# Attention with soft mixture of experts on one core: logits one period later and ahead of the scores, the flip of x inside the values, the first exponentials ahead of the copies of P

## The chip, the core and the metric

The kernel runs on one core of a Trainium2 chip. The core has a matrix engine (TensorE, PE in the profile; its weight loads are PEld), three engines for elementwise work (VectorE is DVE, ScalarE is ACT, GpSimd is POOL), and SyncE (SP), which here only issues transfers. Each engine runs its own queue in order; the engines wait for each other by semaphores. Matrix products land in PSUM, whose banks are few and are used in turns. The metric is the time of one execution in microseconds, as the median of several; all times below are in microseconds unless marked.

## The reference

Windowed causal attention over 8 batches, 8 heads, 576 positions of 64 features, then a soft mixture of 8 experts with 4 slots each over the 4608 tokens of 512 features:

```python
scores = scale * q @ k.T;  scores = where((rel >= 0) & (rel < 128), scores - slope[h] * abs(rel), -1e9)
attn = exp(scores - max);  attn /= sum(attn) + 1e-9
x = (attn @ v)                       # rows (b, s), columns (h, d): 4608 x 512
logits = x @ phi                     # 4608 x 32
d = exp(logits - logits.max(0));  d /= d.sum(0) + 1e-9
slot_input = d.T @ x                 # 32 x 512
slot_out[e] = maximum(slot_input[e] @ w1[e], 0) @ w2[e]
c = exp(logits - logits.max(1)); c /= c.sum(1) + 1e-9
out = c @ slot_out
```

## The kernel before

Attention is cut into 36 tiles, numbered k, of 128 query positions, in two groups g = 0 and 1 of 64, for all 8 heads in four pairs. `tiles[k]` is (b, t); t = 0 is the first tile of a batch. Such a tile sees fewer keys (its scores are shorter) and has no second part in its values. They are k = 0, 4, 9, 13, 18, 22, 27 and 35.

One loop runs over k. Every engine's order is the order in which this loop writes its instructions (`manual_schedule`); nothing is moved by a scheduler. The loop is software-pipelined: in period k TensorE works on tiles k-1, k-2, k-3 and k+1. The steps, by the names of the code:

- `scores(k+1, g)`: slope rows (L233) and products of q and k (L246) into the PSUM tile of group g.
- `chain(k, g)` on VectorE: `merge` (L260), `rowmax` (L267), `bias` (L272); it makes `nb`, the bias of the exponentials.
- `expo(k, g)` on ScalarE: four exponentials (L284) that write P of group g to `p4s[g]`.
- `flip(k-1, g)`: four transposes of P (L303) into bank a for g = 0 and bank b for g = 1. In the text, "flips of P" are the two together.
- `take(k-1, g)` on ScalarE: the copy of the flipped P from that bank (L306). `split(k-1, g)` on GpSimd then makes its two masked parts with four selects (L319, L322).
- `values(k-2)`: the first part (L335) multiplies the main blocks of P with v into banks e and o; the second part (L345) adds the corner blocks and closes the sums.
- `x_store(k-2)` on VectorE: row sums, reciprocal, product (L356, L357, L359); writes one of six x tiles.
- `x_flip(k-3)`: four transposes of x (L365) into bank a, the bank that the flipped P of group 0 is copied out of. `x_keep(k-3)` on ScalarE copies them out (L368) to one of four tiles.

Every four tiles make a round q of the mixture. It is spread over the periods by `do(when, k, ...)`, which puts a step at a named place of period k: `logits` (L375, bank b) of the four kept tiles, `token_copy` on ScalarE (L381), `token_max` on VectorE (L386, L388, L390), `token_exp` on ScalarE (L397, L402); a period later `token_sum` (L408), `token_flips` on TensorE (L416, `dp`), `token_keep` on ScalarE (L422, `dn`), `slot_sum` on TensorE (L428, `ap`), `slot_add` on VectorE (L438); `slots_max` and `slots_norm` give small VectorE steps (L450 to L463) to a list of fillers, of which up to four are taken at the end of each period, ahead of the next chain; `slots_exp` is on ScalarE (L455). The places in a period come in the order turn, turn2, keep, x_keep, mid, post, act, dve, late.

After the loop the last tiles are finished, and the experts' two layers and the output follow; the change leaves that part as it was.

Of the kernel before, what the change touches and what calls it, by code (L numbers as in the profile page):

```python
# [25 lines left out]
NPAIR = H // 2  # L26
# [6 lines left out]
NQ = NTT // 4  # L33
# [32 lines left out]
def tile_attn_softmoe(  # L66
# [82 lines left out]
    st = {}  # L149
    last = B - 1  # L150

    def order(b):
        return (1, 2, 3, 4, 0) if b == last else range(4 + b % 2)

    tiles = [(b, t) for b in range(B) for t in order(b)]
# [9 lines left out]
    def bank(tag, shape, name):  # L165
        return ps_1.tile(shape, F32, tag=tag, name=name)
# [84 lines left out]
    def window(k, g, us, o, w):  # L251
        s = st[k, g]
        if isinstance(us, int):
            return s["parts"][us // 2][:, us % 2, o:o + w]
        if s["s4"] is None:
            return s["parts"][us.start // 2][:, :, o:o + w]
        return s["s4"][:, us, o:o + w]

    def merge(k, g, us=ALL):
        nc.vector.copy_predicated(  # L260
            window(k, g, us, 0, KB), bc(mask_le, 1, len(range(4)[us])), window(k, g, us, P, KB))
# [12 lines left out]
    def corner(k, g, par):  # L274
        return par if tiles[k][1] == 4 else g ^ par

    def expo(k, g, us=ALL):
        s = st[k, g]
        s["p4"] = p4s[g]
        for u in range(4)[us]:  # L280
            dst = s["p4"][:, u].rearrange("p (a w) -> p a w", a=2)
            if corner(k, g, u // 2):
                dst = dst[:, ::-1]
            nc.scalar.activation(  # L284
                dst, window(k, g, u, 0, P).rearrange("p (a w) -> p a w", a=2), AF.Exp,
                bias=s["nb"][:, u:u + 1], scale=SCALE)
# [3 lines left out]
    def filler():  # L290
        if fillers:
            fillers.pop(0)()

    def chain(k, g):
        merge(k, g)
        rowmax(k, g)
        bias(k, g)
# [7 lines left out]
    def take(k, g, copy):  # L305
        copy(pas[k % 2][:, g].rearrange("p a j m -> p (a j m)"), st[k, g]["pt"].rearrange("p u w -> p (u w)"))  # L306
# [18 lines left out]
    def values(k, to=None):  # L325
        b, t = tiles[k]
        x = st["x", k] = to or [bank(tag, [P, NPAIR, VD], "xp") for tag in ("e", "o")]
        for j in range(NPAIR):
            for par in range(2):
                for g in range(2):  # L330
                    if t == 4:
                        v = (v3_even, v_slot[b, 3])[g]
                    else:
                        v = v_slot[b, t - 1 + g if t else 0]
                    nc.tensor.matmul(  # L335
                        x[par][half[g], j], lhsT=pas[k % 2][:, g, par, j], rhs=v[:, par, j],
                        start=(j == 0), stop=(t == 0 and j == NPAIR - 1))
        if t == 0:
            return
        for j in range(NPAIR):  # L340
            for par in range(2):
                for g in range(2):
                    rows = half[corner(k, g, par)]
                    v = (v4_even, v4_odd)[g] if t == 4 else v_slot[b, t - g]
                    nc.tensor.matmul(  # L345
                        x[par][half[g], j], lhsT=pps[k % 2][rows, g, j], rhs=v[rows, par, j],
                        start=False, stop=(j == NPAIR - 1))
# [181 lines left out]
    def do(when, k, fn, *a):  # L529
        todo.setdefault((when, k), []).append((fn, a))  # L530

    def run(when, k):
        for fn, a in todo.pop((when, k), []):
            fn(*a)
# [30 lines left out]
            load_v_tails(b + 1)  # L565

    for q in range(NQ - 1):
        k = 4 * q + 3
        do("post", k + 3, logits, q)
        do("act", k + 3, token_copy, q)  # L570
        do("dve", k + 3, token_max, q)
        do("late", k + 3, token_exp, q)
        do("dve", k + 4, token_sum, q)
        do("turn2", k + 4, token_flips, q)
        do("keep", k + 4, token_keep, q)
        do("mid", k + 4, slot_sum, q, "b")
        do("dve", k + 4, slot_add, q)
        do("dve", k + 4, later, slots_max, q)
        do("act", k + 5, slots_exp, q)
        do("dve", k + 5, later, slots_norm, q)  # L580
    for k in range(n - 3):
        do("turn", k + 3, x_flip, k)
        do("x_keep", k + 3, x_keep, k)
# [1 line left out]
    with tc.manual_schedule(engines=ORDERED):  # L585
        scores(0, 0)
        scores(0, 1)
        loads(0)
        for k in range(n):
            if k:  # L590
                chain(k, 0)
            else:
                for us in (LO, HI):
                    merge(k, 0, us)
                    rowmax(k, 0, us)
                    bias(k, 0, us)
                    expo(k, 0, us)
            chain(k, 1)
            if k:
                flip(k - 1, 0, "a")  # L600
                flip(k - 1, 1, "b")
                run("turn", k)
                run("turn2", k)
            if k:
                take(k - 1, 0, nc.scalar.copy)
                split(k - 1, 0)
                load_weights_at(k, 1)
                take(k - 1, 1, nc.scalar.copy)
                split(k - 1, 1)
                load_weights_at(k, 2)  # L610
                expo(k, 0)
            run("keep", k)
            expo(k, 1)
            run("x_keep", k)
            if k >= 2:
                values(k - 2)
                after_values(k - 2)
            run("mid", k)
            if k + 1 < n:
                scores(k + 1, 0)  # L620
                scores(k + 1, 1)
                loads(k + 1)
            if k == n - 2:
                load_weight()
            run("post", k)
            if k >= 2:
                x_store(k - 2)
            run("act", k)
            run("dve", k)
            run("late", k)  # L630
            for _ in range(4):
                filler()

        ka, kb, kc = n - 3, n - 2, n - 1
        lp = free[3]
        idle = inp.bitcast(BF16)[:, 0:512]

        def spin(m):
            if "spin" not in st:
                st["spin"] = bank("o", [P, 512], "spin")  # L640
            for _ in range(m):
                nc.tensor.matmul(st["spin"], lhsT=idle[:, 0:P], rhs=idle, start=True, stop=True)

        for _ in range(3):
            load_weight()
        nc.gpsimd.memset(inp, 0.0)
        flip(kc, 0, "a")
        flip(kc, 1, "b")
        take(kc, 0, nc.scalar.copy)
        take(kc, 1, nc.vector.tensor_copy)  # L650
        x_flip(ka)
        x_keep(ka)
        values(kb)
        for _ in range(5):
            load_weight()
        values(kc, [x.rearrange("p (j d) -> p j d", d=P)[:, :, 0:VD] for x in (free[0], free[2])])
        x_store(kb)
        run("act", n)
        run("dve", n)
        x_store(kc, (0,))  # L660
        x_store(kc, (1,))
        drain()
        for _ in range(2):
            load_weight()
        spin(1)
        turn(0, "a", free[1])
        x_flip(kb, bank("b", [P, DM], "xq"))
        x_keep(kb)
        spin(1)
        x_flip(kc, None, range(0, 2))  # L670
        x_flip(kc, None, range(2, 4))
        x_keep(kc, nc.scalar.copy, slice(0, 2))
        x_keep(kc, nc.vector.tensor_copy, slice(2, 4))
        logits(final, range(3), to=lp)
        logits(final, range(3, 4))
        spin(2)
        load_weight()
        load_weight()
        token_max(final, lp[:, 0:P])
        lane_rows()  # L680
        turn(1, "v", free[1])
        spin(1)
        token_exp(final, lp[:, 0:P])
        lane_exp()
        token_flips(final, (1,))
        token_keep(final, nc.vector.tensor_copy, slice(0, 1))
        token_sum(final)
        spin(1)
        lane_flip()
        slot_sum(final, "e")  # L690
        lane_keep()
        nc.scalar.copy(lg[:, 0:P], lp[:, 0:P])
        load_weight()
        load_weight()
        for cols in (slice(0, DM // 2), slice(DM // 2, DM)):
            slot_add(final, cols)
        spin(3)
        for part in range(2):
            slot_inputs(part)
            inputs_keep(part)  # L700
        lane_sum()
        lane_norm()
        token_flips(final, (0,))
        token_keep(final, nc.scalar.copy, slice(1, 2))
        assert not todo and loaded[0] == NW + len(place), (todo, loaded, len(place))
# [232 lines left out]
```

## Time and profile before

| what | us |
|---|---|
| median of 3 runs (lowest, highest) | 291.5 (290.72, 293.64) |
| the profiled execution's own time | 293.59 |
| its span, first to last instruction | 291.9 |
| TensorE busy in the span | 253.2 |
| VectorE, ScalarE, GpSimd busy | 178.9, 158.2, 97.6 |

The granted TensorE clock is 0.994 of full speed over the span. In the page, a group of instructions is shown by line, engine, operation, and out<-in by the program's names; in a timeline row the columns are start, duration, engine, line, operation, names and shapes, how many instructions are merged into the row, and in brackets the engine's idle time before it with the instruction that ended it. A row of the view of waits gives the total, the number of times and the longest. A row of the view by windows gives the stretch, its length, then each engine's busy time in the order PE, PEld, DVE, ACT, POOL, the clock, the transfers' share and rate. The engines' lines in the rows are those of the kernel before.

### The profile page before, as it was taken

How to read it: one execution, taken by the hardware profiler on the slowest of the kernel's cores; microseconds unless marked ns; L12 is line 12 of the kernel's file. 1: busy time of each engine (PE TensorE's matmuls, PEld its weight loads, DVE VectorE, ACT ScalarE, POOL GpSimd, SP SyncE). 2: the span in 40 equal slices, each digit the busy share in tenths (PEclk: the TensorE clock that was granted, in tenths of full speed). 3: DMA queues.
4: the chain of work that ended last, by engine and by line, in shares of the span. 5: the costliest groups of instructions: out<-in, count | busy, mean ns of one | idle time of the engine just before them, and what ended most of it. 6: DMA issues, size and time to landing. Idle time of an engine off the chain costs nothing.

```text
span 291.9 us, 12240 instructions
## 1 busy us (share of the span) xinstructions
PE 253.2 (87%) x5088; PEld 183.5 (63%) x5088; DVE 178.9 (61%) x550; ACT 158.2 (54%) x481; POOL 97.6 (33%) x269
## 2 busy tenths in 40 slices
PE   7688898988989897898899989989979889999980
PEld 3466776776777586666667757767766532566640
DVE  3566566775794875589478577657865741224461
ACT  2567756666755776656667566866565201013350
POOL 0046344541660566045417541645544001000000
PEclk9999999999999999999999999999999999999997
DMA  6769975788688477668776858855755999998895
GB/s 177 233 223 273 387 255 170 257 248 269 197 288 285 143 252 236 213 199 268 266 246 189 277 178 260 261 186 154 246 168 183 307 395 305 409 372 308 342 384 234
DMA packets 30715, 74.74 MB, mean 256 GB/s; under 512 B 3650, under 2 KB 5698, under 8 KB 30660
## 3 DMA queue, kind: packets, MB, share of 16 engines
q1 hardware_dynamic: 29940, 73.48, 75.5%
q8 instruction: 40, 0.66, 0.9%
q10 hardware_dynamic: 720, 0.48, 0.6%
q14 instruction: 15, 0.12, 0.1%
HBM read 64.51 MB, written 9.44 MB: 253 GB/s over the span
## 4 chain that ended last, share of the span: by engine, by line
PE 64%; DVE 14%; ACT 14%; issue 4%; DMA 1%; ACTq 0%; DVEq 0%
PE s L246 11%; PE xp L335 10%; PE xq L365 6%; ACT area L306 6%; PE op L772 5%; PE xp L345 5%; ACT area L284 5%; PE hp L736 5%; PE pt L303 5%; PE s L233 4%; PE po L793 4%; DVE nb L267 3%; PE lp L375 3%; PE ap L428 3%; DVE s L260 2%
## 5 line engine op out<-in xcount | busy, mean ns | idle before, releaser
L284 ACT ACTIVATE area<-s,nb 128x128 f32<-128x128 f32 x288 | 81.3, 393 | 9.5 <-DVE nb L272 8.2
L322 POOL TENSOR_SCALAR_AFFINE_SELECT area<-area 64x256 f32<-64x256 f32 x112 | 46.4, 414 | 116.1 <-ACT area L306 110.5
L306 ACT COPY area<-pt 128x512 f32<-128x512 f32 x71 | 38.0, 585 | 46.8 <-PE pt L303 46.0
L246 PE MATMUL s<-kq 64*64 64x192 f32 (+2 forms) x1088 | 53.7, 314 | 0.8 <-DMA kq<-k_t 0.8
L267 DVE TENSOR_REDUCE nb<-s 128x4 f32<-128x512 f32 (+1 forms) x73 | 49.9, 684 | 2.6
L319 POOL TENSOR_SCALAR_AFFINE_SELECT area<-area 64x256 f32<-64x256 f32 x112 | 46.1, 412 | 7.5
L246 PEld LDWEIGHTS s<-kq 64*64 64x64 f32 x1088 | 40.2, 138 | 3.8 <-DMA kq<-k_t 1.4
L335 PE MATMUL xp<-va,area 128*64 128x66 f32 x1120 | 40.9, 225 | 1.1 <-issue 1.1
L335 PEld LDWEIGHTS xp<-va,area 128*64 128x64 f32 x1120 | 35.7, 137 | 7.2 <-issue 4.0
L303 PE MATMUL pt<-unit_r,area 128*128 128x128 f32 x288 | 39.7, 280 | 0.6 <-DVE acc L438 0.6
L365 PE MATMUL xq<-unit_r,xs 128*128 128x128 f32 x144 | 23.7, 286 | 18.1 <-ACT area L306 17.0
L303 PEld LDWEIGHTS pt<-unit_r,area 128*128 128x128 f32 x288 | 30.7, 141 | 10.8 <-issue 7.9
L260 DVE COPY_PREDICATED s<-cst,s 128x256 f32<-128x256 int32 (+1 forms) x73 | 30.7, 420 | 9.1 <-PE s L246 8.9
L356 DVE TENSOR_SCALAR rs<-xp 128x4 f32<-128x4 f32 x70 | 8.7, 161 | 39.8 <-PE xp L345 36.4
L233 PE MATMUL s<-ramp 64*64 64x384 bf16 x288 | 26.5, 342 | 6.5 <-ACT area L284 5.6
L365 PEld LDWEIGHTS xq<-unit_r,xs 128*128 128x128 f32 x144 | 15.3, 141 | 26.2 <-ACT area L306 24.8
L359 DVE TENSOR_TENSOR xs<-xp,rs 128x256 f32<-128x256 f32 x70 | 26.5, 420 | 1.2
L368 ACT COPY xs<-xq 128x512 f32<-128x512 f32 (+1 forms) x36 | 22.7, 631 | 1.1 <-PE xq L365 1.0
L233 PEld LDWEIGHTS <-ramp 64*64 64x64 bf16 x288 | 11.6, 107 | 17.3 <-issue 15.8
L799 DVE COPY ob<-po 128x384 f32<-128x384 f32 x24 | 12.3, 553 | 13.1 <-PE po L793 12.5
L345 PE MATMUL xp<-va,area 64*64 64x66 f32 x896 | 19.6, 224 | 0.0
L799 ACT COPY ob<-po 128x384 f32<-128x384 f32 x24 | 10.3, 482 | 13.6 <-PE po L793 13.6
(112 smaller groups left out, 254.5 us busy)
## 6 DMA issues: line engine op xcount, KB each, us to landing
w<-w SPq DMA_DIRECT2D x49, 512.0 KB, 5.5
va<-v_n SPq DMA_DIRECT2D x36, 264.0 KB, 4.8
out<-ob SPq DMA_DIRECT2D x24, 384.0 KB, 4.1
kq<-q_t SPq DMA_DIRECT2D x35, 256.0 KB, 3.8
kq<-k_t SPq DMA_DIRECT2D x32, 256.0 KB, 4.3
xs<-w SPq DMA_DIRECT2D x5, 512.0 KB, 6.5
area<-w SPq DMA_DIRECT2D x4, 512.0 KB, 8.2
kt<-k_t SPq DMA_DIRECT2D x4, 384.0 KB, 5.2
```

The costliest lines, as they stand in the source:

```text
L233: nc.tensor.matmul(parts[par][half[c], :, 0:WIN], lhsT=slope[rows, c], rhs=steps[rows, 0 if t else 1 + g], start=True, stop=False)
L246: nc.tensor.matmul(parts[par][half[c], jh, KB * o:WIN], lhsT=qt[rows, j], rhs=keys, start=False, stop=(jh == 1))
L260: nc.vector.copy_predicated(window(k, g, us, 0, KB), bc(mask_le, 1, len(range(4)[us])), window(k, g, us, P, KB))
L267: nc.vector.tensor_reduce(s["nb"][:, 4 + us.start:4 + us.stop], window(k, g, us, 0, P), axis=AX.X, op=ALU.max, negate=True)
L284: nc.scalar.activation(dst, window(k, g, u, 0, P).rearrange("p (a w) -> p a w", a=2), AF.Exp, bias=s["nb"][:, u:u + 1], scale=SCALE)
L303: nc.tensor.transpose(s["pt"][:, u], s["p4"][:, u], ident)
L306: copy(pas[k % 2][:, g].rearrange("p a j m -> p (a j m)"), st[k, g]["pt"].rearrange("p u w -> p (u w)"))
L319: nc.gpsimd.affine_select(dst, pa, [[0, NPAIR], [-1, KB]], ALU.is_gt, 0.0, base=0, channel_multiplier=1)
L322: nc.gpsimd.affine_select(dst, pa, [[0, NPAIR], [1, KB]], ALU.is_ge, 0.0, base=0, channel_multiplier=-1)
L335: nc.tensor.matmul(x[par][half[g], j], lhsT=pas[k % 2][:, g, par, j], rhs=v[:, par, j], start=(j == 0), stop=(t == 0 and j == NPAIR - 1))
L345: nc.tensor.matmul(x[par][half[g], j], lhsT=pps[k % 2][rows, g, j], rhs=v[rows, par, j], start=False, stop=(j == NPAIR - 1))
L365: nc.tensor.transpose(st["xq", k][:, P * j:P * j + P], xns[k % NXN][:, P * j:P * j + P], ident)
```

## The change

Three edits in the loop:

1. `values` is cut in two functions. The first part now stands directly behind the flips of P; `x_flip` (and `token_flips`) follow it, and then the second part, `values_ex`. `x_keep` moves behind the place "mid".
2. `expo(k, 0)` is written ahead of both `take(k-1, g)` in place of behind them.
3. For the rounds q = 0 to 6 every step is one period later, and `logits` goes from "post" (behind the scores) to "mid" (ahead of them). Round 7 keeps its periods and its place.

```diff
+    def values_ex(k):
+        b, t = tiles[k]
+        x = st["x", k]
+        for j in range(NPAIR if t else 0):
...
     for q in range(NQ - 1):
-        k = 4 * q + 3
-        do("post", k + 3, logits, q)
-        do("act", k + 3, token_copy, q)
...
+        k = 4 * q + 6 + (q < NQ - 2)
+        do("mid" if q < NQ - 2 else "post", k, logits, q)
+        do("act", k, token_copy, q)
...
                 flip(k - 1, 1, "b")
-                run("turn", k)
-                run("turn2", k)
+            if k >= 2:
+                values(k - 2)
+            run("turn", k)
+            run("turn2", k)
             if k:
+                expo(k, 0)
                 take(k - 1, 0, nc.scalar.copy)
                 split(k - 1, 0)
                 load_weights_at(k, 1)
                 take(k - 1, 1, nc.scalar.copy)
                 split(k - 1, 1)
                 load_weights_at(k, 2)
-                expo(k, 0)
             run("keep", k)
             expo(k, 1)
-            run("x_keep", k)
             if k >= 2:
-                values(k - 2)
+                values_ex(k - 2)
                 after_values(k - 2)
             run("mid", k)
+            run("x_keep", k)
             if k + 1 < n:
                 scores(k + 1, 0)
...
         values(kb)
+        values_ex(kb)
```

The changed file has two more lines above the lines named here, so L345 is L347 there, L365 is L367, L368 is L370, L375 is L377.

TensorE, an ordinary period; the rows are line, operation, out<-in and shape, with how many follow each other (`pt` is the flipped P, `xq` the flipped x, `xp` the values, `s_0` and `s_1` the scores of the two groups). One piece of the difference:

```order
 L246 MATMUL s_1_87<-kq 64x192 x8
 L303 MATMUL pt<-unit_r,area 128x128 x8
-L365 MATMUL xq<-unit_r,xs 128x128 x4
-L335 MATMUL xp<-va,area 64x66 x16
-L345 MATMUL xp<-va,area 64x66 x16
+L335 MATMUL xp<-va,area 64x66 x16
+L367 MATMUL xq<-unit_r,xs 128x128 x4
+L347 MATMUL xp<-va,area 64x66 x16
 L233 LDWEIGHTS ramp
```

The flip of x stood between the flips of P and the values; it now stands between the values' two parts.

ScalarE, an ordinary period and the start of the next one, before (`s_0`, `s_1`: exponentials of group 0 and 1; `area<-pt`: the two copies of P; `xs<-xq`: x_keep):

```order
L306 COPY area<-pt 128x512 x2
L284 ACTIVATE area<-s_0_86,nb 128x128 x2
L284 ACTIVATE area<-s_0_86,nb 128x2x64 x2
L284 ACTIVATE area<-s_1_87,nb 128x2x64 x2
L284 ACTIVATE area<-s_1_87,nb 128x128 x2
L368 COPY xs<-xq 128x512
```

and now:

```order
L284 ACTIVATE area<-s_0_86,nb 128x128 x2
L284 ACTIVATE area<-s_0_86,nb 128x2x64 x2
L306 COPY area<-pt 128x512 x2
L284 ACTIVATE area<-s_1_87,nb 128x2x64 x2
L284 ACTIVATE area<-s_1_87,nb 128x128 x2
L370 COPY xs<-xq 128x512
```

The two copies went from ahead of the exponentials of group 0 to behind them.

ScalarE, a round of the mixture, now (`lg<-lp`: the logits' copy, `lg,sb` and `al`: token_exp, `dn<-dp`: token_keep); before, the first copy row stood directly behind `al` and ahead of the exponentials of `s_0`:

```order
L370 COPY xs<-xq 128x512
L383 COPY lg<-lp 128x128
L399 ACTIVATE lg,sb<-lg,nm 128x128
L404 ACTIVATE al<-fine,nm 128x1
L284 ACTIVATE area<-s_0_86,nb 128x128 x2
L284 ACTIVATE area<-s_0_86,nb 128x2x64 x2
L306 COPY area<-pt 128x512 x2
L424 COPY dn<-dp 128x256
```

The logits' copy and its exponentials keep their places between x_keep and the next period's work; what follows them is now the exponentials of group 0 and not the copies.

More of the change, by code (lines that the diff above doesn't have):

```diff
@@ L337, in values @@
                         start=(j == 0), stop=(t == 0 and j == NPAIR - 1))
-        if t == 0:
-            return
-        for j in range(NPAIR):
+    def values_ex(k):
+        b, t = tiles[k]
+        x = st["x", k]
+        for j in range(NPAIR if t else 0):
             for par in range(2):
@@ L567, in tile_attn_softmoe @@
     for q in range(NQ - 1):
-        k = 4 * q + 3
-        do("post", k + 3, logits, q)
-        do("act", k + 3, token_copy, q)
[L571 to L580, printed above, removed]
+        k = 4 * q + 6 + (q < NQ - 2)
+        do("mid" if q < NQ - 2 else "post", k, logits, q)
+        do("act", k, token_copy, q)
+        do("dve", k, token_max, q)
+        do("late", k, token_exp, q)
+        do("dve", k + 1, token_sum, q)
+        do("turn2", k + 1, token_flips, q)
+        do("keep", k + 1, token_keep, q)
+        do("mid", k + 1, slot_sum, q, "b")
+        do("dve", k + 1, slot_add, q)
+        do("dve", k + 1, later, slots_max, q)
+        do("act", k + 2, slots_exp, q)
+        do("dve", k + 2, later, slots_norm, q)
     for k in range(n - 3):
```

## The prediction

> **What bounds the kernel now.** I read the page first, then the waits, then the stretches of one group of four tiles, then the timeline inside them. All steps below are from the start of one instruction group to the start of the next, in us.
>
> The page gives TensorE most of the span. The view of waits gives who waits for whom (total, times, longest): TensorE's flip of x (`x_flip`) waits for ScalarE's copies of P (`take`), and ScalarE's copies wait for TensorE's flips of P.
>
> ```profile
> PE 253.2 (87%) x5088; PEld 183.5 (63%) x5088; DVE 178.9 (61%) x550; ACT 158.2 (54%) x481; POOL 97.6 (33%) x269
> ACT area L306 <- PE pt L303: 46.0, 27, 2.8
> PE xq L365 <- ACT area L306: 17.0, 33, 1.3
> ```
>
> The view by windows, cut at the starts of `x_flip` (which stands once in each period from k = 3 to 35), gives the four stretches of one group: with logits at the end, with slot sums, with the normalising of the slots, plain. The last row is from the first `x_flip` (k = 3) to the last in the loop (k = 35).
>
> ```profile
> 187.04:194.37 7.33, 6.04 (x148) 4.96 (x149) 3.45 (x14) 4.46 (x16) 3.41 (x9) 1.00 0.89 291
> 194.37:201.07 6.70, 6.40 (x127) 4.50 (x127) 5.21 (x16) 3.90 (x13) 3.40 (x9) 1.00 0.48 135
> 201.07:206.38 5.31, 5.02 (x117) 4.16 (x117) 3.73 (x14) 3.84 (x13) 3.41 (x9) 1.00 0.48 143
> 206.38:211.88 5.50, 5.21 (x116) 4.18 (x116) 4.72 (x15) 3.83 (x12) 3.40 (x9) 1.00 0.76 250
> 23.04:218.59 195.55, 173.84 (x3847) 136.76 (x3847) 137.44 (x431) 127.84 (x398) 88.89 (x241) 1.00 0.74 236
> ```
>
> A group takes 24.84 and TensorE is busy in 22.67 of it. The timeline of the third stretch shows the order that makes its 5.31:
>
> ```profile
> 200.43 1.07 ACT L306 COPY area<-pt 128x512 f32<-128x512 f32 x2 [2.80 <-PE pt L303]
> 201.07 0.66 PE L365 MATMUL xq<-unit_r,xs 128*128 128x128 f32 x4 [0.29 <-ACT area L306]
> 201.08 0.41 POOL L322 TENSOR_SCALAR_AFFINE_SELECT area<-area 64x256 f32<-64x256 f32 x1 [2.76 <-ACT area L306]
> 201.65 1.15 PE L335 MATMUL xp<-va,area 128*64 128x66 f32 x32
> 202.74 0.70 PE L345 MATMUL xp<-va,area 64*64 64x66 f32 x32
> 203.25 0.34 PE L233 MATMUL s<-ramp 64*64 64x384 bf16 x4
> 203.40 0.67 ACT L368 COPY xs<-xq 128x512 f32<-128x512 f32 x1
> 203.47 0.25 DVE L356 TENSOR_SCALAR rs<-xp 128x4 f32<-128x4 f32 x2 [1.31 <-PE xp L345]
> 203.87 0.40 ACT L455 ACTIVATE ln<-ln 128x128 f32<-128x128 f32 x1
> 204.07 0.34 PE L233 MATMUL s<-ramp 64*64 64x384 bf16 x4
> 204.61 0.41 POOL L322 TENSOR_SCALAR_AFFINE_SELECT area<-area 64x256 f32<-64x256 f32 x1
> 204.66 0.28 DVE L460 TENSOR_REDUCE cs<-ln 128x4 f32<-128x128 f32 x1
> 204.99 0.85 PEld L303 LDWEIGHTS pt<-unit_r,area 128*128 128x128 f32 x8 [0.28 <-issue]
> 205.60 0.42 DVE L260 COPY_PREDICATED s<-cst,s 128x256 f32<-128x256 int32 x1
> ```
>
> TensorE: x_flip to values .58, values' first part to second 1.09, second part to scores .51, scores .82 and .92, flips of P to the next x_flip 1.39 (at 206.38). Without its wait of .29 that is 5.02. The chain of VectorE and ScalarE runs beside it and ends in time, because ScalarE copies P before it takes up the exponentials. So TensorE and the small wait behind the copy set an ordinary period.
>
> **Copies behind the first exponentials.** The first copy of P now stands in ScalarE's queue behind the four exponentials of group 0 of the next tile, and these need VectorE's chain of that group. The rows for that link, and then the timeline around logits and slot sums:
>
> ```profile
> 106.31 0.42 DVE L260 COPY_PREDICATED s<-cst,s 128x256 f32<-128x256 int32 x1
> 107.75 1.14 ACT L284 ACTIVATE area<-s,nb 128x128 f32<-128x128 f32 x4 [0.23 <-DVE nb L272]
> ...
> 117.63 1.08 PE L375 MATMUL lp<-xs,phi 128*32 128x128 f32 x32
> 118.78 0.27 ACT L381 COPY lg<-lp 128x128 f32<-128x128 f32 x1 [3.41 <-PE lp L375]
> 119.66 0.42 DVE L260 COPY_PREDICATED s<-cst,s 128x256 f32<-128x256 int32 x1
> 120.43 1.05 ACT L306 COPY area<-pt 128x512 f32<-128x512 f32 x2
> 121.04 0.66 PE L365 MATMUL xq<-unit_r,xs 128*128 128x128 f32 x4 [1.29 <-ACT area L306]
> 121.37 1.15 ACT L284 ACTIVATE area<-s,nb 128x128 f32<-128x128 f32 x4
> 121.53 0.43 PE L416 MATMUL dp<-unit_r,lg 128*128 128x128 f32 x2
> 121.89 1.15 PE L335 MATMUL xp<-va,area 128*64 128x66 f32 x32
> 122.38 0.40 ACT L422 COPY dn<-dp 128x256 f32<-128x256 f32 x1
> 123.61 1.07 PE L428 MATMUL ap<-xs,dn 128*32 128x512 f32 x8
> 123.74 0.25 DVE L356 TENSOR_SCALAR rs<-xp 128x4 f32<-128x4 f32 x2 [1.46 <-PE xp L345]
> 124.60 0.36 PE L233 MATMUL s<-ramp 64*64 64x384 bf16 x4
> 124.93 0.21 DVE L408 SCALAR_TENSOR_TENSOR fine<-fine,al,sb 128x1 f32<-128x1 f32 x1
> 126.24 0.42 DVE L260 COPY_PREDICATED s<-cst,s 128x256 f32<-128x256 int32 x1
> ```
>
> This closes a ring through four engines' queues that was open before. x_flip needs bank a, so it waits for the copy; the values' second part is now behind x_flip; `x_store` on VectorE needs that second part; the next chain is behind x_store in VectorE's queue; the exponentials need the chain; the copy is behind the exponentials. Its length in an ordinary period: x_flip to second part .58 (taken from x_flip to values, the nearest row: four transposes and one change of array shape), second part to x_store .73 (202.74 to 203.47), x_store to the next VectorE group 1.19 (203.47 to 204.66), chain to exponentials 1.44 (106.31 to 107.75), four exponentials to the next ScalarE copy 1.01 (121.37 to 122.38), copy to x_flip .64 (200.43 to 201.07): **5.59**.
>
> **x_flip between the values' parts.** TensorE alone would come round in .58 + .51 + .82 + .92 for x_flip to flips of P, then 8 transposes .85 and .17 for the change of shape, then the first part 1.01 and at most .28 (the gap before the flips, 204.99): 5.14. So the move hides 1.29 of the copy's lateness, but the ring is .45 longer than that, and x_flip waits again: what was late .29 is now late .45. The added change of array shape has no row of its own. The link from x_flip to the second part lies in the ring; its bounds are .42 with no gap (over 31 stretches 5.0 less) and .69 with the .28 gap (3.4 more), and I take .58, the row with the same weights before it. The gap from the first part to x_flip lies under the wait and costs nothing; if that wait went, it would cost up to .28.
>
> The Trainium skill (TensorEngine Tiling (Array Packing), Tiling Modes, Key Properties) says that changing the tiling mode, not just the tile, drains TensorE; this speaks against the change, since each period gets one more such change. The gaps in the trace (.17, .28) agree with it in kind; by it the sum stays as below, and with no drain at that place it would be .16 x 31 = 5.0 less.
>
> **GpSimd.** Its eight selects per tile end 4.59 after the first copy starts (200.43 to 204.61 + .41), and the next values' first part needs them. With the copy at x_flip - .64 that is 3.95 + .1 for the signal, so the first part may start at 4.05 and x_flip 1.29 later, at 5.34. That is under 5.59, and shows only where the ring is shorter (k = 6).
>
> **Logits a period later, before the scores.** Removed: the wait of 1.29 before x_flip (.29 + 1.0) behind the logits' copy and exponential on ScalarE, 8 times before, now 7 of them. Added: logits stand between second part and scores, `x_keep` on ScalarE waits for them since it overwrites their input, the logits' copy is behind x_keep, `token_max` on VectorE behind that copy, and the next chain behind token_max. Ring: .58, then .63 to the logits (as for slot sums: 121.89 to 123.61 less 1.09), 1.15 to their end (117.63 to 118.78), x_keep .47 (203.40 to 203.87), copy to chain .88 (118.78 to 119.66), 1.44, 1.01, .64: 6.80 against 7.33 before. Where the tile in the values is the first of its batch it has no second part, and it is .63 less, 6.17 (k = 11 and 15).
>
> **What VectorE does between x_store and the next chain** was beside TensorE's work before and is in the ring now. Slot sums: x_flip to token flips .49, to second part .36, .73, x_store 1.19, `token_sum`, `slot_add` and two fillers 1.31 (124.93 to 126.24), 1.44, 1.01, .64: 7.17 against 6.70. x_store's multiply there now waits for the slot sum that reads the tile it overwrites; if for the first of four, nothing, if for all, .5: I take nothing, as the tile is the first one's. Normalising: 5.59 and .94 for four fillers (204.66 to 205.60): 6.53 against 5.31. Plain: 5.59 against 5.50.
>
> **Sum.** 31 stretches from k = 3 to 34: 9 plain or without extras x 5.59 = 50.3; k = 6, 5.34; logits 5 x 6.80 + 2 x 6.17 = 46.3; slot sums 7 x 7.17 = 50.2; normalising 7 x 6.53 = 45.7: 197.9. The stretch from k = 34 keeps its logits behind scores of 1.11:
>
> ```profile
> 214.07 0.34 PE L233 MATMUL s<-ramp 64*64 64x384 bf16 x4
> 215.18 1.08 PE L375 MATMUL lp<-xs,phi 128*32 128x128 f32 x32
> ```
>
> .58 + .51 + 1.11 + 1.15 + .88 + 1.44 + 1.01 + .64 = 7.3. Together 205.2 against 195.55: +9.7. At the two ends the first part of the values only changes sides of an x_flip (+1.0 before the first, -1.09 behind the last): -.1. The profiled execution took 293.59 (span 291.9 and 1.7 around it), so it becomes 303.2; it was 2.1 above the median of 291.5, so I expect **301.1**. Loads, weights and the tail of experts are untouched.
>
> **Rivals.** (a) TensorE stays the pace. If the chain were ready .45 earlier in an ordinary period and 1.4 earlier in a normalising one, x_flip would find its copy done, and a group would be 4 x 5.14 + .27 (token flips) + 1.11 (slot sums: .63 + .99 - .51) + 1.11 (logits alike) = 23.05 against 24.84. Over 31/4 groups that is -13.9: 278 us. The 1.29 and .29 rows speak for it, the ring against: every link of it is a queue's order or a measured step. It decides from the ring falling below 5.14. The Trainium skill (Perfetto Trace Analysis, Optimization Strategy) says to find the gaps on the busiest engine and make what they wait for start sooner, by which this change should gain; no run here shows yet whether it does.
> (b) Little changes. With no gap behind x_flip (-5.0) it is 296; another .1 off each of 31 turns (-3.1), for instance in the step from exponentials to copy, which I have from the copy of another tile (122.38), gives 293. For it speaks that no row shows x_flip ahead of the second part; against it that the two nearest rows have gaps.
> (c) Worse still: the .5 at slot sums (7 x .5 = 3.5) and .11 more per change of shape (31 x .11 = 3.4): 308. For it speaks the added wait itself, against it that only one of the four slot sums reads the tile.
>
> **Chances.** A measurement of this kernel tells 1% from no change. Forecast with its own range of 296 to 306: .68; (c) .10; (b) .10; (a) and parts of it .12. So faster .12, same .10, slower .78. The range for 8 in 10 takes in (b) and (c): 290 to 308.
>
> **What would show it.** Right: ScalarE's copies no longer wait for TensorE (46.0 falls near 0), its first exponentials wait for the bias instead, x_flip's wait for the copy grows from 17.0 to 20 to 30, and the normalising stretch is above 6.3. The logits stretch shrinks by about .5 in any case. Wrong: x_flip's wait under 10, or VectorE starting a chain sooner than 1.9 after the values' second part in a plain period.

## The result, and the profile after

| | median us (lowest to highest, runs) | profiled execution | its span |
|---|---|---|---|
| before | 291.83 (290.72 to 293.64, 4) | 293.59 | 291.9 |
| after | 308.56 (308.02 to 308.88, 4) | 308.68 | 306.9 |

The change makes the kernel slower: ratio 1.0565, 95% interval 1.0508 to 1.0622. The forecast was 301.1 with a range up to 308.0: the direction and the ring came out, the size did not, and the time lies .56 above the range. Medians here and below are over all runs of a kernel and ratios over its fast ones, which matters for two kernels below: without the runs of a slower state of the chip, 275.12 would be 274.34, and 309.88 would be 308.62.

The page and the view of waits of the kernel after (engine and line waited for, total us, times, longest):

```profile
PE 257.8 (84%) x5086; PEld 186.3 (61%) x5088; DVE 175.9 (57%) x550; ACT 158.4 (52%) x481; POOL 97.6 (32%) x269
L306 ACT COPY area<-pt 128x512 f32<-128x512 f32 x71 | 38.8, 614 | 1.5 <-PE pt L303 1.5
ACT area L284 <- DVE nb L272: 58.7, 27, 3.2
PE xq L367 <- ACT area L306: 31.9, 30, 1.9
DVE xs L361 <- PE ap L430: 7.5, 7, 2.6
```

The copies of P, which waited 46.0 for TensorE, now wait 1.5: by the time ScalarE reaches them the flips are long done. ScalarE waits 58.7 for the bias of the exponentials instead, and x_flip waits 31.9 for the copies where it waited 17.0. The last row is new: x_store's product waits for the slot sums.

The view by windows of the kernel after, cut at the starts of x_flip: one group from k = 23 (logits, slot sums, normalising, plain), then k = 3 to 35 as before.

```profile
151.42:158.23 6.81, 6.16 (x149) 4.95 (x149) 4.53 (x17) 4.60 (x16) 0.00 (x0) 1.00 1.02 376
158.23:165.92 7.69, 5.84 (x95) 3.93 (x95) 4.55 (x12) 4.00 (x13) 3.40 (x9) 1.00 0.50 169
165.92:172.56 6.64, 5.03 (x116) 4.18 (x116) 4.48 (x15) 3.83 (x13) 3.40 (x9) 1.00 0.46 141
172.56:178.31 5.75, 4.76 (x116) 3.96 (x116) 3.68 (x11) 3.63 (x12) 3.40 (x9) 1.00 0.72 254
23.55:233.44 209.89, 175.90 (x3849) 138.30 (x3847) 135.08 (x431) 127.37 (x398) 88.46 (x241) 0.99 0.68 221
```

The loop from the first x_flip to the last takes 209.89 against 195.55, 14.3 of the 15.0 that the span grew by; the start (+.5) and the tail (+.2) hold the rest. The last stretch of that group, by the timeline, shows the ring link by link:

```profile
172.56 0.66 PE L367 MATMUL xq<-unit_r,xs 128*128 128x128 f32 x4 [1.61 <-ACT area L306]
173.15 0.56 PEld L347 LDWEIGHTS xp<-va,area 64*64 64x64 f32 x32 [0.17 <-issue]
173.91 0.25 DVE L358 TENSOR_SCALAR rs<-xp 128x4 f32<-128x4 f32 x2 [1.85 <-PE xp L347]
175.10 0.42 DVE L260 COPY_PREDICATED s<-cst,s 128x256 f32<-128x256 int32 x1
176.57 0.89 PEld L335 LDWEIGHTS xp<-va,area 128*64 128x64 f32 x26 [0.42 <-POOL area L322]
176.63 1.15 ACT L284 ACTIVATE area<-s,nb 128x128 f32<-128x128 f32 x4 [2.12 <-DVE nb L272]
177.65 1.09 ACT L306 COPY area<-pt 128x512 f32<-128x512 f32 x2
178.31 0.42 PEld L367 LDWEIGHTS xq<-unit_r,xs 128*128 128x128 f32 x4 [0.85 <-ACT area L306]
```

x_flip to second part .59, to x_store .76, to the chain 1.19, to the exponentials 1.53, to the copy 1.02, to x_flip .66: 5.75. Each engine starts at once when the one before it has ended, and VectorE, ScalarE and TensorE each sit idle for part of every turn (1.85, 2.12, and .85 in the last row). GpSimd's selects delay the values (.42 at 176.57), but the weight loads of x_flip still wait .85 behind them for the copy, so the selects set nothing here.

### The profile page after: what moved, and what is told of

Read it like the earlier page. It is cut to its first block, busy times and chain, and to the rows that moved or that the text cites. A ratio compares the mean times of both kernels' runs of the same rounds, so it can differ in the third digit from the quotient of the medians.

```text
span 306.9 us, 12376 instructions
## 1 busy us (share of the span) xinstructions
PE 257.8 (84%) x5086; PEld 186.3 (61%) x5088; DVE 175.9 (57%) x550; ACT 158.4 (52%) x481; POOL 97.6 (32%) x269
## 4 chain that ended last, share of the span: by engine, by line
PE 49%; DVE 23%; ACT 17%; issue 7%; POOL 1%; DMA 1%; ACTq 0%; DVEq 0%; POOLq 0%
ACT area L284 10%; PE xq L367 7%; PE xp L347 6%; DVE nb L267 6%; PE op L777 5%; ACT area L306 5%; PE s L246 5%; PE hp L741 5%; PE po L798 4%; DVE xs L361 4%; PE ap L430 3%; PE pt L303 3%; DVE s L260 3%; PE lp L377 3%; PE xp L335 2%
## 5 line engine op out<-in xcount | busy, mean ns | idle before, releaser
L284 ACT ACTIVATE area<-s,nb 128x128 f32<-128x128 f32 x288 | 83.9, 389 | 75.5 <-DVE nb L272 58.7
L322 POOL TENSOR_SCALAR_AFFINE_SELECT area<-area 64x256 f32<-64x256 f32 x112 | 46.3, 414 | 130.7 <-ACT area L306 125.1
L246 PE MATMUL s<-kq 64*64 64x192 f32 (+2 forms) x1088 | 54.8, 319 | 0.7 <-DMA kq<-k_t 0.7
L267 DVE TENSOR_REDUCE nb<-s 128x4 f32<-128x512 f32 (+1 forms) x73 | 49.9, 684 | 2.6
L367 PE MATMUL xq<-unit_r,xs 128*128 128x128 f32 x144 | 23.7, 287 | 31.9 <-ACT area L306 31.9
L319 POOL TENSOR_SCALAR_AFFINE_SELECT area<-area 64x256 f32<-64x256 f32 x112 | 46.1, 412 | 7.8 <-POOL w L146 0.3
L335 PE MATMUL xp<-va,area 128*64 128x66 f32 x1120 | 42.9, 226 | 1.3 <-POOL area L322 0.8
L335 PEld LDWEIGHTS xp<-va,area 128*64 128x64 f32 x1120 | 37.0, 137 | 8.2 <-issue 5.2
L306 ACT COPY area<-pt 128x512 f32<-128x512 f32 x71 | 38.8, 614 | 1.5 <-PE pt L303 1.5
L367 PEld LDWEIGHTS xq<-unit_r,xs 128*128 128x128 f32 x144 | 15.3, 141 | 36.3 <-ACT area L306 36.0
L370 ACT COPY xs<-xq 128x512 f32<-128x512 f32 (+1 forms) x36 | 22.4, 621 | 5.5 <-PE lp L377 4.7
L347 PE MATMUL xp<-va,area 64*64 64x66 f32 x896 | 20.2, 228 | 0.0
L347 PEld LDWEIGHTS xp<-va,area 64*64 64x64 f32 x896 | 16.2, 137 | 4.8 <-issue 4.7
L233 PEld LDWEIGHTS <-ramp 64*64 64x64 bf16 x288 | 10.5, 110 | 13.8 <-issue 13.1
```

What stands on the lines that cost most here:

```text
L246: nc.tensor.matmul(parts[par][half[c], jh, KB * o:WIN], lhsT=qt[rows, j], rhs=keys, start=False, stop=(jh == 1))
L267: nc.vector.tensor_reduce(s["nb"][:, 4 + us.start:4 + us.stop], window(k, g, us, 0, P), axis=AX.X, op=ALU.max, negate=True)
L284: nc.scalar.activation(dst, window(k, g, u, 0, P).rearrange("p (a w) -> p a w", a=2), AF.Exp, bias=s["nb"][:, u:u + 1], scale=SCALE)
L319: nc.gpsimd.affine_select(dst, pa, [[0, NPAIR], [-1, KB]], ALU.is_gt, 0.0, base=0, channel_multiplier=1)
L322: nc.gpsimd.affine_select(dst, pa, [[0, NPAIR], [1, KB]], ALU.is_ge, 0.0, base=0, channel_multiplier=-1)
L335: nc.tensor.matmul(x[par][half[g], j], lhsT=pas[k % 2][:, g, par, j], rhs=v[:, par, j], start=(j == 0), stop=(t == 0 and j == NPAIR - 1))
```

## The experiments

Theory R is the ring of the prediction. Its rival S: the time comes from cutting the values in two, with one more change of array shape on TensorE in each period. The first four kernels split the change into its edits. An interval of the ratio that lies wholly below 1 is a gain clear of noise. The table has the medians, the ratio to the runs of the kernel before on the same chip, and the time from the first x_flip (k = 3) to the last (k = 35).

| kernel | us | ratio (95%) | x_flip 3 to 35 |
|---|---|---|---|
| edits 1 and 3 (copies first) | 282.91 | 0.970 (0.963 to 0.977) | 184.56 |
| edit 2 alone | 362.67 | 1.242 (1.234 to 1.251) | 266.67 |
| edit 1 alone | 284.40 | 0.976 (0.968 to 0.983) | 184.75 |
| edit 3 alone | 287.36 | 0.984 (0.977 to 0.991) | 189.57 |
| edits 1 and 2 | 314.58 | 1.077 (1.071 to 1.082) | 216.27 |
| the change, fillers behind the chains | 297.27 | 1.017 (1.013 to 1.021) | 199.31 |
| the change, exponentials between the copies | 287.49 | 0.984 (0.980 to 0.988) | 188.56 |
| the change, seven x tiles | 303.12 | 1.043 (1.036 to 1.049) | 207.45 |
| edits 1 and 3, fillers behind the chains | 275.12 | 0.938 (0.929 to 0.948) | 175.21 |
| the same, seven x tiles | 274.38 | 0.945 (0.937 to 0.952) | 175.91 |

**Copies first (edit 2 undone).**

```diff
             if k:
-                expo(k, 0)
                 take(k - 1, 0, nc.scalar.copy)
...
                 load_weights_at(k, 2)
+                expo(k, 0)
```

> The changed kernel with edit 2 undone: the copies of P ahead of the first exponentials again; x_flip stays inside the values, logits stay a period later. Theory R (the ring x_flip, second part, x_store, chain, exponentials, copy, x_flip sets the period): the ring is open, TensorE sets the pace at about 5.14 in a plain period, 277 to 284 us, and x_flip's wait for ScalarE falls under 5 us in total. Theory S (the added change of array shape and the split of the values cost the time): still above 300 us.

282.91, as R expects, and the weight loads of x_flip wait only .9 in all for the copy; S is out: all of the shape changes are still there. The timeline shows what they cost, at the flip of x and the second part of k = 26, and what holds TensorE now:

```profile
152.13 1.01 PEld L335 LDWEIGHTS xp<-va,area 128*64 128x64 f32 x32 [0.17 <-issue]
153.21 0.42 PEld L367 LDWEIGHTS xq<-unit_r,xs 128*128 128x128 f32 x4
153.80 0.56 PEld L347 LDWEIGHTS xp<-va,area 64*64 64x64 f32 x32 [0.17 <-issue]
155.68 0.36 PE L233 MATMUL s<-ramp 64*64 64x384 bf16 x4 [0.67 <-ACT area L284]
```

x_flip starts 1.08 after the first part, whose weight loads take 1.01, with no gap listed; behind it the gap is .17, and it waits for nothing. The Trainium skill (TensorEngine Tiling (Array Packing), Tiling Modes, Key Properties) has every change of mode drain TensorE; the .17 agrees in kind, and the .07 before x_flip shows how little such a change may cost. The scores of group 1 wait .67 for exponentials.

**Edit 2 alone.**

```diff
             if k:
+                expo(k, 0)
                 take(k - 1, 0, nc.scalar.copy)
...
-                expo(k, 0)
```

> The kernel before with edit 2 alone: first exponentials ahead of both copies, x_flip directly behind the flips of P. Theory R: the ring now holds the whole of the values (1.09 more than in the changed kernel), 6.68 in a plain period, and logits behind the scores give a ring of about 9: 330 to 345 us. Theory S: near 292 us, since no array shape is added.

362.67: over both, so R's sign holds, and its size is short. Windows of this kernel: the first stretch, k = 3, then two stretches of 3.41 one behind the other.

```profile
23.78:30.51 6.73, 4.38 (x117) 3.73 (x117) 3.60 (x11) 3.62 (x12) 3.38 (x9) 1.00 0.87 274
152.15:155.56 3.41, 0.84 (x6) 0.62 (x6) 1.96 (x5) 2.42 (x9) 0.00 (x0) 1.00 0.64 241
155.56:158.97 3.41, 3.41 (x69) 3.00 (x72) 0.21 (x2) 1.89 (x6) 0.00 (x0) 0.50 0.11 14
```

At full clock a plain stretch takes 6.73, where 6.68 was reckoned. But TensorE waits so much here that the clock was granted at half for 3.41 at a time, 17 such spells between the first x_flip and the last (one of 6.8), and here TensorE's values are in the ring: the later plain stretches take 6.73 to 6.80 without a spell (k = 13, 21, 25) and 7.07 to 8.09 with one (k = 9, 17, 29, 33). That accounts for the direction of the excess; how much of it the spells hold in all was not separated.

**Edit 1 alone.** The copies are ahead of the exponentials and the round of the mixture keeps its periods:

```diff
-        k = 4 * q + 6 + (q < NQ - 2)
-        do("mid" if q < NQ - 2 else "post", k, logits, q)
+        k = 4 * q + 3
+        do("post", k + 3, logits, q)
...
```

> The kernel before with edit 1 alone: x_flip between the values' parts, x_keep behind mid; copies first, logits on their old place. Theory R: the wait of .29 goes and most of the 1.29 behind the logits is covered by the values' first part: 277 to 284 us. Theory S: above 300 us.

284.40, .4 above what R expects and far from S. The flip of x inside the values is a gain by itself.

**Edit 3 alone.** To the kernel before, the round's table of the change and `run("x_keep", k)` behind `run("mid", k)`.

> The kernel before with edit 3 alone (and x_keep behind mid, which it needs, since logits now read what x_keep overwrites): logits a period later and ahead of the scores. Theory R: 1.0 of wait less in each of 7 rounds, no ring closed: 283 to 287 us. Theory S says nothing of this edit: it adds no array shape in a plain period, so the same 283 to 287.

287.36, .36 above the range expected and 4.5 under the kernel before beside it. So two of the three edits gain alone (both intervals lie below 1), and the third costs more than both gain.

**Edits 1 and 2**, the round's table as before:

> The changed kernel with edit 3 undone (logits on their old period, behind the scores). Theory R: the stretch with logits has a ring of .58 + .51 + .82 + .92 + 1.15 + .88 + 1.44 + 1.01 + .64 = 7.95 in place of 6.8, the slot-sum stretch loses its .5 of wait and has 7.2: 310 to 317 us, more if the granted clock drops oftener. If edit 3 did harm in the changed kernel: under 307 us.

314.58, as R expects: with the ring closed, edit 3 is still worth 6.0 (314.58 - 308.56). The stretch with logits, k = 18, by windows:

```profile
117.24:125.22 7.98, 7.01 (x192) 5.83 (x196) 4.85 (x16) 4.87 (x16) 5.31 (x15) 1.00 0.62 212
```

7.98 against 7.95 reckoned from the links. The full-clock slot-sum stretches with a second part take 7.23 (k = 19, 31), as expected without the wait: a period earlier, x_store writes a tile that the slot sums do not read.

**Fillers behind the chains**, in the changed kernel:

```diff
             chain(k, 1)
+            for _ in range(4):
+                filler()
...
             run("late", k)
-            for _ in range(4):
-                filler()
```

> The changed kernel with the four fillers of a period (the small steps of slots_max and slots_norm) behind both chains of the next period in place of ahead of them. Theory R: they leave the ring, .94 less in 7 normalising stretches and .6 less in 7 slot-sum stretches: 10.8 less, 296 to 300 us. Without a ring through VectorE's queue: 308 us as they are the same work.

297.27, in the middle of R's range. The same VectorE work costs 11.3 more ahead of the chain than behind it, where a normalising stretch takes 5.73 (k = 25) and a plain one 5.64 (k = 30). This is the plainest evidence for the ring: nothing was changed but its place in VectorE's queue.

**Exponentials between the two copies**, in the changed kernel:

```diff
-                expo(k, 0)
                 take(k - 1, 0, nc.scalar.copy)
                 split(k - 1, 0)
                 load_weights_at(k, 1)
+                expo(k, 0)
                 take(k - 1, 1, nc.scalar.copy)
```

> The changed kernel with the first exponentials between the two copies of P: the copy of group 0, on which x_flip waits, is first again. Theory R: the ring is open just as with both copies first, and ScalarE still uses some of its idle time: 280 to 286 us. If the order of all copies against exponentials mattered (a later second copy): near 300 us.

287.49: the ring is open, but the time is 1.5 above the range and 4.6 above both copies first. The second copy and the second exponentials come later here; which of the two costs the 4.6 was not tried.

**Seven x tiles**, in the changed kernel: x_store wrote the tile that the first slot sum of the same period reads.

```diff
-NXN = 6
+NXN = 7
...
-    inp = cpool.tile([P, NX + NS - SW], F32, name="inp")
...
+    inp = kt[:, 0:NX + NS - SW]
...
```

> The changed kernel with seven x tiles in place of six (the cleared input tile of the experts moves into a key tile that is done by then), so that x_store no longer overwrites a tile that the slot sums of the same period read. If the term I set at nothing (x_store's wait for the slot sums) is the .5 in each of 7 slot-sum stretches: 304 to 306 us, those stretches 7.2 in place of 7.7, and no wait of x_store's product for the slot sums. If it is not on the ring: unchanged at 308 to 309.

In this first form the last weights came over a tile of x that round 8 still used, so its output is not the kernel's, and its tail took longer (309.88 in all): only its loop can be read. Its slot-sum stretches were 6.8 to 7.3. The second form puts these weights one tile further:

> The changed kernel with seven x tiles, as before, but with the late weights placed only over x tiles that are done by then. If x_store's wait for the slot sums is the half microsecond in each of 7 slot-sum stretches: 304 to 306 us, those stretches 7.2 in place of 7.7, and the time behind the last x_flip back at 73. If not: 308 to 309 us.

303.12: somewhat under the range. The slot-sum stretches of k = 24 and 28 by windows, first of this kernel, then k = 28 of the changed one (its k = 24 stands above, 158.23:165.92):

```profile
158.03:164.86 6.83, 5.85 (x94) 3.93 (x95) 4.55 (x12) 4.00 (x13) 3.51 (x9) 1.00 0.60 195
184.02:191.24 7.22, 6.40 (x126) 4.49 (x126) 5.30 (x19) 3.98 (x13) 0.00 (x0) 1.00 0.90 268
```

```profile
185.11:192.78 7.67, 6.41 (x127) 4.50 (x127) 5.31 (x19) 4.01 (x13) 0.00 (x0) 1.00 0.86 257
```

.45 less in a usual one and .86 less where the tile in the values has no second part, where x_store could start before the slot sums. So the wait that I set at nothing is real. Over the seven stretches it is 53.8 against 49.8, 4.0, and the ratios to the kernel before on the same chip, 1.0565 and 1.0427, differ by as much (4.0). The rest of the 5.4 between the medians isn't in these stretches, and this kernel's loop even has two plain stretches of 6.5 and 6.9 that the changed one hasn't, the second with a spell of half clock in it (144.26 to 147.67).

What x_store waits for stands in the timeline of the changed kernel at k = 24, and in the windows of the slot sums' line alone (TensorE's busy time with the number of its instructions, then clock and transfers):

```profile
159.61 1.07 PE L430 MATMUL ap<-xs,dn 128*32 128x512 f32 x8 [0.46 <-ACT dn L424]
160.69 0.76 DVE L361 TENSOR_TENSOR xs<-xp,rs 128x256 f32<-128x256 f32 x2 [2.61 <-PE ap L430]
```

```profile
159.60:159.64 0.04, 0.03 (x4) 1.00 0.02 0
160.66:160.70 0.04, 0.02 (x3) 1.00 0.00 0
```

The four slot sums, of two instructions each, run side by side: four instructions start within .04, and behind 160.66 only one of the last four has ended, the one of the first slot sum; the other three end by 160.68. The trace's semaphore events tell which one lets x_store go. The first slot sum signals at 160.67, the product starts at 160.69, and the signal behind the last slot sum comes at 160.75; in all seven stretches the product starts .02 behind the first signal and .05 ahead of the last. So x_store waits for the first slot sum alone, and this one ends no sooner than the others.

**Towards a better kernel.** Edits 1 and 3 with the fillers behind the chains, and then seven x tiles as well:

> The kernel with edit 2 undone (282.9 us) and the fillers behind both chains. There the scores of group 1 still wait .7 in some periods for the second exponentials, which wait for the chains behind the fillers. If that is what is left over TensorE's own work: 279 to 281 us. If TensorE alone is the pace: 282 to 284 us.

> The same with seven x tiles as well. x_store's wait for the slot sums delays the next chain only in slot-sum stretches: 278 to 281 us if the chains still end last there, the same as the kernel with six tiles if they do not.

275.12 and 274.38: 7.8 less than copies first, where 2 to 4 were expected, and nothing more from the seventh tile (the two differ by less than either's spread of runs). A plain stretch (k = 30) of the first, by windows:

```profile
173.32:178.27 4.95, 4.95 (x121) 4.18 (x117) 4.52 (x16) 3.57 (x12) 3.33 (x10) 1.00 0.87 277
```

TensorE is busy for all of its 4.95: this is its own pace. Copies first alone had 5.74 there, since the fillers delayed the second exponentials, and these the scores.

## Why the forecast had the direction and missed the size

**Right.** The ring through x_flip, second part, x_store, chain, exponentials and copy bounds the changed kernel: undoing edit 2 alone opens it (282.91), and shifting the fillers moves the time by their length (297.27). The logits stretch was reckoned at 6.80 and took 6.81; the normalising one 6.53 and 6.64; the plain one 5.59 and 5.75 (here the step from chain to exponentials was 1.53, not 1.44, and the others up to .03 longer). The three signs named in advance came: the copies' wait fell to 1.5, ScalarE waits for the bias, x_flip's wait grew (to 31.9, just above the 20 to 30).

**The step that failed.** "If for the first of four, nothing, if for all, .5: I take nothing, as the tile is the first one's". The tile and the wait are the first one's, but the price isn't nothing: the four slot sums run side by side, the first ends 1.05 after their start and the last .02 later, so waiting for the first costs what waiting for all does. The seven slot-sum stretches took 53.8 in place of 50.2, and with the wait removed 49.8; the two of them without a second part (k = 20 and 24) took 6.83 then, not 7.17. Without that wait the time is 303.12, inside the range and 2.0 from the forecast. I had its size as part of a worse rival at .10.

**The rest of the 7.5** between 301.1 and 308.56, by terms of the sum: plain stretches 51.4 in place of 50.3 (+1.1), normalising 46.1 for 45.7 (+.4), logits 46.2 for 46.3 (-.1), k = 6 4.96 for 5.34 (-.4), the last 7.4 for 7.3 (+.1): with the slot sums +4.7. The two ends gave +.7 where -.1 was reckoned (+.8); a spell of half clock falls behind the last x_flip (233.72 to 237.13), and what it holds of the .8 was not separated. The last 2.0 is no event in the kernel: I took off the 2.1 by which the profiled execution of before lay above its median, and that of after lies only .1 above its own.

**Rivals.** (a), TensorE as the pace, is what edits 1 and 3 give without edit 2; its 278 compares with 282.91, and with 275.12 once the fillers are out of the way too. Its price of a TensorE round, 5.14, was too high by .19: the step from first part to x_flip took 1.08 in the kernel with copies first (152.13 to 153.21), not 1.29. The Trainium skill's advice (Perfetto Trace Analysis, Optimization Strategy) to make what the busiest engine waits for start sooner held for edit 3 alone, where x_flip's wait for the copy fell from 17.0 to 10.2. Edit 1 gained by having x_flip ask for the copy later (a wait of 1.7), and edit 2 made the copy itself later. (b) did not come. Of (c) the first half came, the second did not: the changes of shape cost .17 and less.

## What to carry to other kernels

Before an instruction is moved up in one engine's queue to fill idle time, follow what it waits for back through the other queues: if that chain comes round to what is now behind it, the idle time was the slack that kept a ring open. Every small instruction on such a ring then costs its full length, so the first cure is to move what has no hurry behind the link, as with the fillers. And where several instructions run side by side, a wait for the first of them costs as much as a wait for all: what counts is when the first one ends, not which one it is.

## What the runs showed of the hardware

The granted clock halved in the middle of the loop, in spells of 3.41. By windows of the changed kernel, the stretch ahead of such a spell, the spell, and the period around it:

```profile
83.54:86.95 3.41, 1.65 (x54) 1.34 (x53) 1.80 (x5) 2.68 (x9) 0.86 (x3) 1.00 0.79 237
86.95:90.36 3.41, 3.41 (x60) 2.48 (x51) 2.79 (x11) 1.16 (x4) 2.58 (x8) 0.50 0.53 173
85.94:92.60 6.66, 6.66 (x117) 5.20 (x117) 4.41 (x15) 3.85 (x13) 3.44 (x10) 0.74 0.72 237
```

TensorE was busy 1.65 of the 3.41 ahead, 48%. Counted over the thirteen traces in such windows (from 24 us to 265 us, on the raster on which the spells stand), 26 windows at full clock were followed by half clock, all with TensorE busy 50% or less; of the more than 800 that were not, three had less than half, 46, 49 and 49.9%. The kernel before never came under 59% and had no such spell in the loop. Here the period of 6.66 is as long as its neighbours of the same kind (6.64 at 165.92), and TensorE had time to spare in the ring; in the kernel with edit 2 alone, stretches with a spell were longer than those without. The Trainium skill (TensorE: Matmul & The Clock Gate, Part 1) gives the same window, 3413 ns, and half rate after an idle window. The length agrees with the trace; the condition differs, since a window that was 48% busy sufficed here.
